# Turning the first chunk of x in two halves, with layer 1 on the first half between

## The chip, the cores and the metric

The kernel runs on one core of a Trainium2 chip. TensorE (PE) multiplies, ScalarE (ACT) and VectorE (DVE) work on tiles in SBUF and PSUM, GpSimd (POOL) makes constants, and SyncE (SP) issues nearly all transfers. The metric is the device time of one execution, in microseconds (us); less is better.

## The reference

A dense layer with GELU and a second dense layer, in bf16, for x of 2048 rows and 448 columns, w1 of 448 x 1792, w2 of 1792 x 448:

```python
h = jnp.einsum("bsd,df->bsf", x, w1) + b1
h = jax.nn.gelu(h, approximate=True)
return jnp.einsum("bsf,fd->bsd", h, w2) + b2
```

## The kernel before

The 2048 rows of x are cut into four chunks of 512, and a chunk into four tiles of 128. For each chunk, layer 1 makes h transposed (features on partitions) in 14 feature tiles of 128, taken two at a time, so in seven pairs; GELU on ScalarE writes it to `g`; and layer 2 multiplies `g` with w2, two row tiles at a time (one at a time at the very end). VectorE adds b2 and SyncE stores.

The contraction over 448 columns is not a multiple of 128. So it is done in slices of 64 rows: TensorE's array is used as two halves of 64 rows, and two matmuls, one for each feature tile of a pair, run side by side on the two halves. A pair of feature tiles lies in one `unit` of PSUM (two banks, one for each tile). `part_a` of a pair takes one 64-row half of three slices for each tile, `part_b` takes the other half, and last the leftover 64 columns (weights `w1r`). Since both parts add to the same bank from different halves of the array, `part_b` waits until the last matmul of `part_a` is done; the function `roll` puts the `part_b` of the pair before between the two. `w1r` is loaded to partitions 64 to 127, and VectorE copies every second feature tile's weights to the lower half (L341).

Every engine has a list of instructions in the order in which the Python code appends them, and it runs that list in order. Waits are semaphores, made out of named events (`after=`, `event=`). SyncE's queue holds, in this order: x of the first chunk (one transfer, L113), the first piece of w1 (feature tiles 0 to 3), `w1r`, the second piece (4 to 7), the third (8 to 13), w2 in two pieces, b2 spread over the partitions, then the other three chunks of x by transposing transfers.

Layer 1 needs x transposed. Chunks 1 to 3 come transposed. The first chunk is turned on TensorE: seven warming matmuls on constants (L158), then for each of four tiles three transposes out of `xn` and one out of `xr`, in which VectorE has put the last 64 columns twice (`twice`, L165). The four transposes of a tile go to one bank, and VectorE or ScalarE copies them to `xT` (L180). All four tiles are turned, then b1 is turned by one more transpose (L187, copied by L189), and only then layer 1 starts. In the first chunk a tile holds the rows p*4+t (so a partition gets four neighbouring rows of x, 3584 bytes), and the stores of that chunk put them back.

The first two pairs of the first chunk run their `part_a` over the columns 0 to 255 and then 256 to 511, which belong to tiles 0 and 1, and 2 and 3; everything else is 512 wide.

```python
for t0 in (0, HC):
    for item in items:
        item[0](t0, t0 + HC)
```

Of the kernel before, what the change touches and what calls it, by code (L numbers as in the profile page):

```python
# [7 lines left out]
BF16 = mybir.dt.bfloat16  # L8
FP32 = mybir.dt.float32


class Program:

# [3 lines left out]
    def __init__(self, nc, es):  # L17
        self.nc, self.es = nc, es
        self.lists = {e: [] for e in self.COMPUTE + ("sync",)}
        self.sems = {e: es.enter_context(nc.semaphore(f"sem_{e}")) for e in self.COMPUTE}  # L20
        self.count = dict.fromkeys(self.COMPUTE, 0)
        self.where = {}

    def op(self, engine, make, after=(), event=None):
        if event is not None:
            self.count[engine] += 1
            self.where[event] = (f"sem_{engine}", self.sems[engine], self.count[engine])
        self.lists[engine].append((make, tuple(after), self.sems[engine] if event else None, 1))

    def dma(self, engine, make, event, after=()):  # L30
        if event not in self.where:
            name = "dma_" + "_".join(str(p) for p in (event if isinstance(event, tuple) else (event,)))
            self.where[event] = (name, self.es.enter_context(self.nc.semaphore(name)), 0)
        name, sem, n = self.where[event]
        self.where[event] = (name, sem, n + 16)
        self.lists[engine].append((make, tuple(after), sem, 16))

    def barrier(self, engine, after):
        self.lists[engine].append((None, tuple(after), None, 0))

    def emit(self):
        for name in self.lists:
            self._run(getattr(self.nc, name), name)

    def _run(self, eng, name):
        seen = {}
        for make, after, sem, inc in self.lists[name]:
            for event in after:
                key, s, value = self.where[event]
                if seen.get(key, 0) < value:  # L50
                    eng.wait_ge(s, value)
                    seen[key] = value
            if make is None:
                continue
            done = make(eng)
            if sem is not None:
                done.then_inc(sem, inc)


def bass_standalone__dense_activation_gelu__prompt_kernel(  # L60
# [21 lines left out]
    NWARM = 7  # L82

    with ExitStack() as es:
        sb = lambda name, shape, dt: es.enter_context(nc.sbuf_tensor(name, shape, dt))
        xT = sb("xT", [P, KT + 1, S], BF16)
# [3 lines left out]
        xn = sb("xn", [P, STC, D], BF16)  # L90
        xr = sb("xr", [P, STC, P], BF16)
        ident = sb("ident", [P, P], BF16)
        junk = sb("junk", [P, 1], BF16)
        b1n = sb("b1n", [P, P], BF16)
        b1_f = sb("b1_f", [P, NFT], FP32)
        b2_bc = sb("b2_bc", [P, D], BF16)
        g = sb("g", [P, NFT, S], BF16)
# [8 lines left out]
        x0v = x2[0:SC, :].rearrange("(p t) d -> p t d", t=STC)  # L106
        o0v = out2[0:SC, :].rearrange("(p t) d -> p t d", t=STC)


        W1CUTS = (0, 4, 8, 14)  # L110

        def load_x():
            pr.dma("sync", lambda e: e.dma_start(xn[:, :, :], x0v[:, :, :]), "x")  # L113
# [16 lines left out]
        load_x()  # L130
        load_w1(0)
        load_w1r()
# [5 lines left out]
        for c in range(1, NSC):  # L138
            for slot, d0 in enumerate((0, P, 2 * P, D - P)):
                pr.dma("sync", lambda e, c=c, slot=slot, d0=d0: e.dma_start(  # L140
                    xT[:, slot, c * SC:(c + 1) * SC], x2[c * SC:(c + 1) * SC, d0:d0 + P], transpose=True), ("xT", c))
# [5 lines left out]
            base=0, pattern=[[-1, P]], channel_multiplier=1), after=["ident0"], event="ident")  # L147
        pr.op("vector", lambda e: e.memset(b1n[:, :], 0.0), event="b1z")  # L148
# [3 lines left out]


        busy = {}

        def warm(n, cols=SC):
            for _ in range(n):
                pr.op("tensor", lambda e: e.matmul(unit[3][:, 1, 0:cols], lhsT=ones_w, rhs=ones_m[:, 0:cols],  # L158
                                                   start=True, stop=True))

        def stage(t):
            return unit[t // 2][:, t % 2, 0:2 * P].bitcast(BF16)

        def twice(t):
            pr.op("vector", lambda e: e.tensor_copy(  # L165
                xr[:, t, :].rearrange("p (two h) -> p two h", two=2),
                xn[:, t, D3:D].unsqueeze(1).broadcast_to([P, 2, H])), after=["x"], event=("xr", t))

        def turn(t, copier):
            for k in range(KT + 1):  # L170
                src = xn[:, t, k * P:(k + 1) * P] if k < KT else xr[:, t, :]
                need = ["ident", "x"] if k < KT else [("xr", t)]
                pr.op("tensor", lambda e, k=k, src=src: e.transpose(  # L173
                    stage(t)[:, k * P:(k + 1) * P], src, ident[:, :]),
                    after=need, event=("xt", t) if k == KT else None)

            def evac(e):
                o = xT[:, :, t * P:(t + 1) * P]
                i = stage(t).rearrange("p (k s) -> p k s", k=KT + 1)
                return e.copy(o, i) if copier == "scalar" else e.tensor_copy(o, i)  # L180

            pr.op(copier, evac, after=[("xt", t)], event=("xT0", t))
            busy[(t // 2, t % 2)] = ("xT0", t)

        def turn_b1():
            b1T = unit[0][:, 1, 0:H].bitcast(BF16)
            pr.op("tensor", lambda e: e.transpose(b1T, b1n[:, :], ident[:, :]),  # L187
                  after=["b1n", "ident", ("xT0", 1)], event="b1T")
            pr.op("vector", lambda e: e.tensor_copy(b1_f[:, :], b1T[:, 0:NFT]), after=["b1T"], event="b1")  # L189
            busy[(0, 1)] = "b1"  # L190
# [3 lines left out]

        order = [2]
# [9 lines left out]
        serial = [0]  # L205

        def fence():
            serial[0] += 1
            return ("half", serial[0])

        def layer1(c, j):
            u = next_unit()
            c0, c1 = c * SC, (c + 1) * SC
            turned = fence()

            def mm(lo, half, k, t0, t1, first, fin, after, event):
                ft = 2 * j + lo
                rows = slice(half * H, (half + 1) * H)
                lhsT = w1_sb[rows, k, ft * P:(ft + 1) * P] if k < KT else w1r[rows, ft * P:(ft + 1) * P]
                pr.op("tensor", lambda e: e.matmul(  # L220
                    unit[u][:, lo, t0:t1], lhsT=lhsT, rhs=xT[rows, k, c0 + t0:c0 + t1], start=first, stop=fin,
                    skip_group_check=c == 0 and j < 2), after=after, event=event)

            def part_a(t0=0, t1=SC):

                need = free(u) if t0 == 0 else []
                need += [("xT0", t) for t in range(t0 // P, t1 // P)] if c == 0 else [("xT", c), ("xTd", c)]
                for k in range(KT):
                    for lo in (0, 1):
                        after = (need if k == 0 else []) + [("w1", w1_of(2 * j + lo))]  # L230
                        mm(lo, lo, k, t0, t1, k == 0 and t0 == 0, False, after,
                           turned if k == KT - 1 and lo and t1 == SC else None)

            def part_b():
                for k in range(KT + 1):
                    for lo in (0, 1):
                        fin = k == KT
                        mm(lo, 1 - lo, k, 0, SC, False, fin, [turned] if k == 0 else ["w1r", "w1rU"] if fin else [],
                           ("h", c, 2 * j + lo) if fin else None)
                for lo in (0, 1):  # L240
                    ft = 2 * j + lo
                    pr.op("scalar", lambda e, lo=lo, ft=ft: e.activation(  # L242
                        g[:, ft, c0:c1], unit[u][:, lo, :], ACT.Gelu_apprx_tanh,
# [3 lines left out]
            return part_a, part_b  # L247

        def store(c, st, after):
            j = c * STC + st  # L250
            dst = o0v[:, st, :] if c == 0 else out2[j * P:(j + 1) * P, :]
            pr.dma("sync", lambda e: e.dma_start(dst, out_sb[:, j, :]), "out", after=after)

        def layer2(c, tiles, last=False):

            u = next_unit()
            split = len(tiles) == 1
            n = DH if split else D
            turned = fence()

            def mm(ft, lo, half, first, fin, after, event):
                st = tiles[0] if split else tiles[lo]
                j = c * STC + st
                rows = slice(half * H, (half + 1) * H)
                d0 = lo * DH if split else 0
                pr.op("tensor", lambda e: e.matmul(  # L266
# [133 lines left out]
```

## Time and profile before

| what | value |
|---|---|
| median of five timed runs | 94.67 us (94.51 to 95.11) |
| the profiled execution | 95.46 us |
| its span, first to last instruction | 94.1 us |
| TensorE busy | 90.2 us, 96% of the span |
| ScalarE busy | 38.0 us, 40% |
| VectorE busy | 12.3 us, 13% |
| DMA engines, mean busy share 0 to 6.88 us | 0.72, 198 GB/s |
| DMA engines, 6.88 to 9.05 us | 1.07, 361 GB/s |

The profile is of one execution, which was slower than the median of the timed ones; the difference between its time and its span lies ahead of the first and behind the last instruction. A line of the profile names the line of the code, the engine, the operation, output and inputs, and its times; "idle before" is how long the engine did nothing just before, and the releaser is what ended that. `w_sb` in the profile stands for both `w1_sb` and `w2_sb` (numbers are dropped from names), `u` for the PSUM units. An instruction of L220 is layer 1, one of L266 layer 2. Matmuls are pipelined, so their lengths overlap; the distance between their starts tells the speed.

### The profile page before, as it was taken

The numbers are of one execution on the slowest core, as the hardware profiler recorded it, in microseconds if no ns is written. First come the engines' busy times: TensorE is split into PE (matmuls) and PEld (weight loads), VectorE is DVE, ScalarE is ACT, GpSimd is POOL, SyncE is SP. The second block draws the span as 40 slices with busy tenths as digits, with TensorE's granted clock in tenths as the row PEclk, the third lists the DMA queues.
The fourth block names the chain that finished last, engine by engine and source line by source line (L and its number), as shares of the span: only waits on it lengthen the run. The fifth ranks groups of instructions, "written<-read, shape, count | busy, mean of one in ns | idle before, by whom it ended". The sixth has DMA issues, their size and how long they took to land.

```text
span 94.1 us, 2049 instructions
## 1 busy us (share of the span) xinstructions
PE 90.2 (96%) x933; PEld 46.6 (50%) x933; DVE 12.3 (13%) x29; ACT 38.0 (40%) x61; POOL 1.1 (1%) x7
## 2 busy tenths in 40 slices
PE   6969999999999999999999999999999999999990
PEld 2446444454554444454544444455544444475890
DVE  0141001000136000000136000000134000000421
ACT  3340878810000878810000878810000878810001
POOL 4000000000000000000000000000000000000000
PEclk9999999999999999999999999999999999999999
DMA  2989999855937100000032000000032000000023
GB/s 58 320 224 367 380 319 68 163 107 113 61 64 196 49 0 0 7 0 0 0 101 89 11 0 0 3 7 0 0 98 88 9 0 7 0 0 7 12 85 98
DMA packets 12260, 7.32 MB, mean 78 GB/s; under 512 B 6940, under 2 KB 12060, under 8 KB 12252
## 3 DMA queue, kind: packets, MB, share of 16 engines
q1 hardware_dynamic: 12224, 7.20, 32.8%
q8 instruction: 7, 0.11, 0.6%
q10 hardware_dynamic: 28, 0.00, 0.0%
q14 instruction: 1, 0.01, 0.0%
HBM read 3.79 MB, written 1.84 MB: 60 GB/s over the span
## 4 chain that ended last, share of the span: by engine, by line
PE 90%; DMA 6%; SPq 0%; DVE 0%; issue 0%
PE u L266 45%; PE u L220 45%; DMA w_sb<-in_w_dram 6%; SPq L113 0%; DVE out_sb L305 0%; PE u L273 0%
## 5 line engine op out<-in xcount | busy, mean ns | idle before, releaser
L242 ACT ACTIVATE g<-u,b_f 128x512 bf16<-128x512 f32 x56 | 35.0, 686 | 41.3 <-PE u L220 41.3
L266 PE MATMUL u<-w_sb,g 64*128 64x448 bf16 (+1 forms) x504 | 43.2, 328 | 0.0
L220 PE MATMUL u<-xT,w_sb 64*128 64x512 bf16 (+1 forms) x348 | 40.9, 369 | 0.9 <-DMA w_sb<-in_w_dram 0.9
L266 PEld LDWEIGHTS u<-w_sb,g 64*128 64x128 bf16 x504 | 24.5, 94 | 18.4
L220 PEld LDWEIGHTS u<-xT,w_sb 64*128 64x128 bf16 x348 | 16.9, 94 | 20.0 <-DMA w_sb<-in_w_dram 1.0
L290 DVE TENSOR_TENSOR out_sb<-u,b_bc 128x448 bf16<-128x448 f32 x14 | 8.1, 620 | 61.3 <-PE u L266 61.3
L220 PE MATMUL u<-xT,w1r 64*128 64x512 bf16 x56 | 10.6, 376 | 0.0
L220 PEld LDWEIGHTS u<-xT,w1r 64*128 64x128 bf16 x56 | 2.7, 94 | 3.3
L308 ACT CAST out_sb<-u 128x224 bf16<-128x224 f32 x1 | 0.3, 346 | 9.2 <-PE u L266 9.2
L158 PE MATMUL u<-const-bfloat16-1.0 128*128 128x512 bf16 x7 | 3.1, 627 | 0.8 <-PEq L385 0.8
L180 ACT COPY xT<-u 128x512 bf16<-128x512 bf16 x2 | 1.2, 586 | 2.2 <-PE u L173 2.2
L158 PEld LDWEIGHTS u<-const-bfloat16-1.0 128*128 128x128 bf16 x7 | 0.9, 138 | 2.1 <-issue 2.1
L151 ACT ACT_TABLE_LOAD x1 | 1.3, 1283 | 1.6 <-DVE b1n L148 1.6
L173 PE MATMUL u<-ident,xn 128*128 128x128 bf16 x12 | 1.8, 302 | 0.1
L173 PEld LDWEIGHTS u<-ident,xn 128*128 128x128 bf16 x12 | 1.3, 139 | 1.0 <-issue 1.0
L361 DVE COPY xT<-xT 64x512 bf16<-64x512 bf16 x3 | 0.9, 289 | 3.8 <-DMA xT<-in_x_dram 3.7
L173 PE MATMUL u<-ident,xr 128*128 128x128 bf16 x4 | 1.1, 283 | 0.0
L357 DVE COPY b_z<-b_bc 1x448 bf16<-1x448 bf16 x1 | 0.3, 268 | 6.5 <-DMA b_bc<-in_b_dram 6.5
L165 DVE COPY xr<-xn 128x128 bf16<-128x128 bf16 x4 | 0.6, 190 | 3.0 <-DMA xn<-in_x_dram 3.0
L180 DVE COPY xT<-u 128x512 bf16<-128x512 bf16 x2 | 0.9, 426 | 0.7 <-PE u L173 0.7
L298 DVE TENSOR_TENSOR out_sb<-u,b_bc 128x448 bf16<-128x448 f32 x1 | 0.6, 625 | 1.7 <-PE u L266 1.7
L341 DVE COPY w1r<-w1r 64x896 bf16<-64x896 bf16 x1 | 0.4, 420 | 1.6 <-DMA w1r<-in_w_dram 1.6
(16 smaller groups left out, 3.4 us busy)
## 6 DMA issues: line engine op xcount, KB each, us to landing
out_dram<-out_sb SPq DMA_DIRECT2D x16, 112.0 KB, 1.7
w_sb<-in_w_dram SPq DMA_DIRECT2D x2, 784.0 KB, 9.7
w_sb<-in_w_dram SPq DMA_DIRECT2D x2, 384.0 KB, 6.0
w_sb<-in_w_dram SPq DMA_DIRECT2D x1, 576.0 KB, 7.4
xn<-in_x_dram SPq DMA_DIRECT2D x1, 448.0 KB, 3.2
w1r<-in_w_dram SPq DMA_DIRECT2D x1, 224.0 KB, 6.1
xT<-in_x_dram SPq DMA_TRANSPOSE x12, 4.2
b_bc<-in_b_dram SPq DMA_DIRECT2D x1, 112.0 KB, 9.0
```

The source lines that it names most:

```text
L151: pr.op("scalar", lambda e: e.activation(junk[:, :], one, ACT.Gelu_apprx_tanh))
L158: pr.op("tensor", lambda e: e.matmul(unit[3][:, 1, 0:cols], lhsT=ones_w, rhs=ones_m[:, 0:cols], start=True, stop=True))
L165: pr.op("vector", lambda e: e.tensor_copy(xr[:, t, :].rearrange("p (two h) -> p two h", two=2), xn[:, t, D3:D].unsqueeze(1).broadcast_to([ ...
L173: pr.op("tensor", lambda e, k=k, src=src: e.transpose(stage(t)[:, k * P:(k + 1) * P], src, ident[:, :]), after=need, event=("xt", t) if k ...
L180: return e.copy(o, i) if copier == "scalar" else e.tensor_copy(o, i)
L220: pr.op("tensor", lambda e: e.matmul(unit[u][:, lo, t0:t1], lhsT=lhsT, rhs=xT[rows, k, c0 + t0:c0 + t1], start=first, stop=fin, skip_group ...
L242: pr.op("scalar", lambda e, lo=lo, ft=ft: e.activation(g[:, ft, c0:c1], unit[u][:, lo, :], ACT.Gelu_apprx_tanh, bias=b1_f[:, ft:ft + 1], s ...
L266: pr.op("tensor", lambda e: e.matmul(unit[u][:, lo, 0:n], lhsT=g[rows, ft, j * P:(j + 1) * P], rhs=w2_sb[rows, ft, d0:d0 + n], start=first ...
L290: pr.op("vector", lambda e, lo=lo, j=j: e.tensor_tensor(out=out_sb[:, j, :], in0=unit[u][:, lo, 0:D], in1=b2_bc[:, :], op=ALU.add), after= ...
L298: pr.op("vector", lambda e: e.tensor_tensor(out=out_sb[:, j, :].rearrange("p (two h) -> p two h", two=2), in0=unit[u][:, :, 0:DH], in1=b2_ ...
L341: pr.op("vector", lambda e: e.tensor_copy(odd(slice(0, H)), odd(slice(H, P))), after=["w1r"], event="w1rU")
L361: pr.op("vector", lambda e, cs=cs: e.tensor_copy(xT[0:H, KT, cs], xT[H:P, KT, cs]), after=[("xT", c + 1)], event=("xTd", c + 1))
```

## The change

The first chunk is turned in two halves. Tiles 0 and 1 of x come as transfers of their own (rows t*128 to t*128+127, 896 bytes for each partition), then the first piece of w1, then tiles 2 and 3 in one transfer. TensorE runs five warming matmuls, turns tiles 0 and 1, runs two more warming matmuls of 256 columns, then `a` of the pairs 0 and 1 on columns 0 to 255, and only then turns tiles 2 and 3. The steps that follow are written out: the other half of the array for these 256 columns (without `w1r`), `a` on columns 256 to 511, the `w1r` step on columns 0 to 255, `a` of pair 2, and then `b` of the pairs 0 and 1 on columns 256 to 511. From pair 3 on the order is as before.

b1 is no longer turned by TensorE: VectorE turns it by four 32x32 block transposes in SBUF and one copy. ScalarE copies tiles 0 and 2, VectorE tiles 1 and 3. The helper `mm` remembers which half of the array last wrote each bank, and makes a matmul of the other half wait for it, bank by bank. Layer 2 of chunks 0 to 2 takes its first parts as feature tiles 0 to 9 of both row-tile pairs, then 10 to 13 of both. The stores of the first chunk write rows in their natural order.

```diff
-    NWARM = 7
+    NWARM = 5
...
-        load_x()
-        load_w1(0)
+        def load_x(t0, t1):
+            pr.dma("sync", lambda e: e.dma_start(
+                xn[:, t0:t1, :], x2[t0 * P:t1 * P, :].rearrange("(t p) d -> p t d", p=P)), ("x", t0))
...
+        load_x(0, 1)
+        load_x(1, 2)
+        load_w1(0)
+        load_x(2, 4)
         load_w1r()
         load_w1(1)
...
+        def turn_b1():
+            for q in range(4):
+                pr.op("vector", lambda e, q=q: e.transpose(
+                    b1t[32 * q:32 * q + 32, :], b1n[:, 32 * q:32 * q + 32]), after=["b1n"], event=("b1t", q))
+            pr.op("vector", lambda e: e.tensor_copy(b1_f[:, :], b1t[:, 0:NFT]),
+                  after=[("b1t", q) for q in range(4)], event="b1")
...
+        def mm(u, lo, half, cols, lhsT, rhs, start, stop, after, event=None, skip=False):
+
+            after = list(after)
+            before = side.get((u, lo))
+            if start:
+                before = None
+            if before is not None and before[0] != half:
+                after.append(before[1])
...
         warm(NWARM)
-        for t, copier in enumerate(("vector", "scalar", "vector", "scalar")):
-            if t % 2 == 0:
-                twice(t)
-                twice(t + 1)
-            turn(t, copier)
+        twice(0)
+        twice(1)
+        turn(0)
+        turn(1)
+        evac_half(0)
+        turn_b1()
+        warm(2, HC)
+        L = [Layer1(0, j) for j in range(NPAIR)]
+        L[0].a(0, HC)
+        L[1].a(0, HC)
+        twice(2)
+        twice(3)
+        turn(2)
+        turn(3)
+        evac_half(1)
...
+        for j in (0, 1):
+            for k in range(KT):
+                L[j].step("b", k, 0, HC)
+        L[0].a(HC, SC)
+        L[1].a(HC, SC)
+        for j in (0, 1):
+            L[j].step("b", KT, 0, HC)
+        L[2].a()
+        L[0].b(HC, SC)
+        L[1].b(HC, SC)
+        for j in range(3, NPAIR):
+            L[j].a()
+            L[j - 1].b()
+        L[-1].b()
...
+            head, tail, every = range(0, 10), range(10, NFT), range(NFT)
+            p = Layer2(c, (0, 1))
+            if c + 1 < NSC:
+                q = Layer2(c, (2, 3))
+                for part in (head, tail):
+                    p.part("a", part)
+                    q.part("a", part)
+                p.part("b", every)
+                q.part("b", every)
```

## The prediction

> **What bounds the kernel now.** I read the chain that ended last first, then the timeline of the start, then the waits.
>
> The chain in order of time (start us, length us, what):
>
> ```profile
> 1.19 5.64 DMA w_sb<-in_w_dram
> 6.83 0.05 issue
> 6.88 10.76 PE u L220 x110
> 17.64 10.59 PE u L266 x112
> 28.24 10.58 PE u L220 x98
> ```
>
> From 6.88 us the chain never leaves TensorE until the last output copy: 85.1 us of matmuls without a hole (a later layer 1 takes 10.58 us, a layer 2 10.59). Only the 6.88 us ahead of them can shrink, and the chain says that they end with the first part of w1. The timeline of that stretch (start, length, engine, line, operation, idle before):
>
> ```profile
> 0.77 3.15 PE L158 MATMUL u<-const-bfloat16-1.0 128*128 128x512 bf16 x7 [0.77 <-PEq L385]
> ...
> 4.03 0.48 PE L173 MATMUL u<-ident,xn 128*128 128x128 bf16 x3
> ...
> 5.81 0.22 PE L187 MATMUL u<-ident,b1n 128*128 128x128 bf16 x1
> 5.88 0.59 ACT L180 COPY xT<-u 128x512 bf16<-128x512 bf16 x1 [0.21 <-PE u L173]
> ...
> 6.88 2.13 PE L220 MATMUL u<-xT,w_sb 64*128 64x256 bf16 x30 [0.86 <-DMA w_sb<-in_w_dram]
> 7.79 0.42 DVE L341 COPY w1r<-w1r 64x896 bf16<-64x896 bf16 x1 [1.56 <-DMA w1r<-in_w_dram]
> ```
>
> TensorE itself is busy until 6.02, then idles 0.86. So the wait for w1 is worth at most 0.86 us while 16 transposes and that of b1 stand ahead of the matmuls. The groups give the price of layer 1's small pieces and what they waited for:
>
> ```profile
> L220 PE MATMUL u<-xT,w_sb 64*128 64x256 bf16 x24 | 1.5, 270 | 0.9 <-DMA w_sb<-in_w_dram 0.9
> ```
>
> The clock: a 128x512 warming matmul starts every 0.43 us and a transpose every 0.107 us until about 5.58; later a pair of 512-wide half-row matmuls starts every 0.216 and a pair of 256-wide ones every 0.109. So the array runs at half speed until 5.58.
>
> One thing decides how to read this: the profiled execution took 95.46 us (94.1 span, 1.36 around it), the median of the timed runs is 94.67, 0.79 less. The landing record of the first w1 piece has 14 of its 16 parts by 4.98 us and two stragglers, 6.09 and 6.84. Without stragglers the matmuls could start at 6.02, 0.86 earlier. That is nearly the whole difference, so I estimate that timed runs are already bound by TensorE's own prologue, not by w1.
>
> **What the Trainium skill says.** "TensorE: Matmul & The Clock Gate", Part 1: the array is at half clock until a free-running window of about 3.4 us has been busy; the trace agrees as to the half speed and the switch at 5.58, 4.8 us after the first matmul. "DMA: Bandwidth & Descriptors", Queues, rings and completion order: each engine takes descriptors in ring order, and a transfer is done only when all its engines are; the stragglers fit. "VectorE: DVE Perf Modes", The three transpose paths: 311 ns for a 128x128 VectorE transpose in 32x32 blocks; no run shows one yet.
>
> **The change, part by part.** I use a marker at which both programs have done the same matmul work: the start of the third pair's first matmuls (20 half-width pairs of layer 1 done, 20 x 0.109 = 2.18 us). Before: 6.88 + 2.18 = 9.06 in the profile, and 6.02 + 2.18 = 8.20 by my estimate for the timed runs. All after the marker is equal work.
>
> *First tiles.* x was 448 KB, 3.2 us to landing. Two tiles of 112 KB come first; a store of 112 KB takes 1.7 us. Bounds for the second tile: 2.9 (issue 1.19 + 1.7) to 3.9 (as before); I take 3.1. Five warming matmuls end at 0.77 + 5 x 0.43 = 2.9. Eight transposes x 0.107 = 0.86: the last starts at 3.85. In before the VectorE copy starts 0.35 after the start of a tile's last transpose and takes 0.43: xT of two tiles is there at 4.63. Matmuls may start at 4.65, against 6.02.
>
> *w1, first piece.* Issued one place later on SyncE (1.65, not 1.19), but with 224 KB less ahead, some 0.7 us of x's transfer: most parts by 4.3, a straggler 5.4 to 6.1. I take 4.65 as the start.
>
> *First half of two pairs.* 6 pairs. Half clock until 5.58 gives 0.93 / 0.215 = 4.3 of them, the other 1.7 cost 0.19: 5.77. The clock costs 0.47 here.
>
> *Turning tiles 2 and 3, now among the matmuls.* Eight transposes that stood in a prologue now stand on the path. At full clock not shown well: between 0.055 (half of 0.107) and 0.107; I take 0.08, so 0.64 (0.44 to 0.86): 6.41. Their x lands behind the first w1 piece, 5.0 to 5.5 without stragglers, covered.
>
> *Then* 6 pairs of the other row half, 0.65: 7.06. VectorE's copy of tile 3 ends at 6.35 + 0.35 + 0.43 = 7.13, so 0.07 of waiting; ScalarE's copy of tile 2 (0.59) is earlier. 6 pairs of the second half: 7.78. The new waits between row halves of one bank: a 256-wide matmul lasts 0.27, three pairs (0.33) lie between for most, so 0 to 0.1; for the second pair's w1r step only one pair lies between: 0.27 + 0.05 - 0.11 = 0.2. Two pairs with w1r, 0.22. Sum 8.2 to 8.3.
>
> *w1r and the second w1 piece.* w1r landed at 7.77 (14 parts by 7.02) and its VectorE copy takes 0.42, needed at about 7.8: ready 7.5 to 8.25. The second piece landed at 8.64 (14 parts by 8.12), needed at 8.2 to 8.3. The same bytes are ahead; x in rows of 896 bytes instead of 3584, and two more issues on SyncE of about 0.45 each, put up to 0.2 to 0.4 on both. Without stragglers this hides, just.
>
> *b1.* Off TensorE: minus 0.1 (one transpose) from the prologue. VectorE gets four block transposes and a copy, by the page's price 0.3 to 0.6 with the copy, ahead of the copies for tiles 2 and 3: 4.63 + 0.5 = 5.1, before tile 2 is needed at 5.77. Hidden; if x comes late it stays hidden too.
>
> *Later.* SyncE's transposing loads and b2 issue up to 0.9 later; the first are needed at 28 us and were there before 18.7: nothing. ScalarE's first GELU comes 0.5 to 1 later than 9.27; it works 1.27 of every 1.51 us, and catches up before layer 2, where the last GELU outputs are needed after 20 feature tiles of work, not 12: nothing. The outputs' rows and the split of layer 2 keep 56 pairs of matmuls and at least four pairs between half switches: nothing.
>
> Sum: marker at 8.25, that is 0.8 below the profiled execution's 9.06 (95.46 - 0.8 = 94.65 profiled) but about equal to the 8.20 that I estimate for the timed runs: 94.67 + 0.05, about 94.7.
>
> **The rivals.**
> *A. As summed, about equal: 94.7* (94.3 to 95.1 for itself). What is won by the earlier start (1.37) is spent: half clock 0.47, transposes 0.64, waits 0.3. Chance 0.43.
> *B. Faster: the timed runs before did wait for w1 as the profile shows*, the 0.79 lies elsewhere, and the new order removes that wait: 94.67 - 0.75 = 93.9; or the clock rises earlier. For it: the chain names w1. Against: no room is left then for the 0.79, and stragglers would delay the new kernel as well (w1 at 6.1, x behind it, marker about 9.2). Chance 0.22.
> *C. Slower: the clock stays down for another window.* The new prologue has holes: before tile 1, and from 4.25 (end of two half warming matmuls) to 4.65 or, with a straggler, to 6.1. If the busy share falls short the switch comes 3.41 later, at 8.99: first half 1.29, transposes 0.86, next 1.29 and most of the next at half speed, marker 9.6: 94.67 + 1.4 = 96.1. It decides when the share in the window ending at 5.58 is too small; the first window (TensorE busy 1.4 of 3.41, 41%) was, the second (97%) was not; mine is about 89%. Against it, then. Chance 0.15.
> *D. Slower: a transfer takes the place of the old wait.* w1r or the second w1 piece lands 0.2 to 0.4 later through small rows and later issues, on top of a landing as the profile had: marker 8.85 to 9.1, 95.3 to 95.6. The change would then not do what it says. For it: data move at 180 to 270 GB/s between 4.5 and 6.5 us, less than later, whatever the order. Chance 0.20.
>
> **Numbers.** 0.5% of 94.67 is 0.47 us, about what a measurement tells from none. Same is A, 0.43; faster B, 0.22; slower C and D, 0.35. The range goes from B to C, 93.9 to 96.1, leaving the far side of each.
>
> **What would show it.** Right: the first L215 matmul starts near 4.65; the transposes of tiles 2 and 3 take about 0.64 between two bursts; the third pair starts at 8.2 to 8.3; no hole after it. C shows as 256-wide pairs every 0.215 us past 6; D as TensorE idle before the third pair or before the w1r step, put down to DMA. A hole in the later chunks, or layer 2 above 10.59 us, would make the sum wrong altogether.

## The result: a little slower, and where the half microsecond went

The changed kernel stands at 1.0059 of the kernel before, 95% interval 1.0033 to 1.0084. On a median of 94.68 us (47 runs) that is 0.56 us, so 95.24 us. Its median over all 28 runs is 96.51 us, but 16 of these took 96.4 us or more (of the kernel before 3 of 47) and lie outside the ratio, by which the text below compares. The profiled execution took 95.65 us with a span of 94.3 (before: 95.46 and 94.1).

The chain that ended last, of the kernel after (start us, length us, what):

```profile
1.65 0.43 SPq L130
2.08 0.04 issue
2.12 4.80 DMA xn<-in_x_dram
6.92 0.05 issue
6.97 0.69 PE u L342 x8
7.65 84.50 PE u L215 x913
```

Before, the chain went through the first piece of w1 until 6.83. Now it goes through tiles 2 and 3 of x, until 6.92, and only after these and their eight transposes does TensorE run without a hole. In this execution the wait was not removed. It was given to another transfer.

The timeline of the same stretch of the kernel after:

```profile
4.32 0.89 DVE L179 STREAM_TRANSPOSE b1t<-b1n 32x32 bf16<-32x32 bf16 x4
...
5.55 0.55 PEld L215 LDWEIGHTS u<-xT,w_sb 64*128 64x128 bf16 x12 [1.67 <-DMA w_sb<-in_w_dram]
5.56 0.83 PE L215 MATMUL u<-xT,w_sb 64*128 64x256 bf16 x12 [1.19 <-DVE b_f L181]
...
6.94 0.30 DVE L335 COPY xr<-xn 128x128 bf16<-128x128 bf16 x2 [1.42 <-DMA xn<-in_x_dram]
...
6.97 0.34 PE L342 MATMUL u<-ident,xn 128*128 128x128 bf16 x3 [0.58 <-DMA xn<-in_x_dram]
...
7.58 1.49 PE L215 MATMUL u<-xT,w_sb 64*128 64x256 bf16 x24
...
9.25 1.17 PE L215 MATMUL u<-xT,w_sb 64*128 64x512 bf16 x12
```

Layer 1 does start earlier, at 5.56 against 6.88. (The page puts the wait of the matmul down to VectorE's bias copy; the code has no such wait there, and the weight load's row names w1, which landed at 5.51.) At 6.39 the first burst of six pairs is over, and TensorE idles for 0.58 us until tiles 2 and 3 have landed. The third pair's first matmul, the prediction's marker, is at 9.25; before it was at 9.06. What follows is the same work in the same time, as a table by stretch shows (start:end, length, busy time of TensorE and its weight loads, ...), first the kernel after, then the one before:

```profile
6.20:6.97 0.77, 0.19 (x5) 0.01 (x1) 0.03 (x1) 0.00 (x0) 0.00 (x0) 1.00 1.03 241
6.97:7.58 0.61, 0.61 (x8) 0.44 (x9) 0.27 (x2) 0.12 (x1) 0.00 (x0) 1.00 1.09 339
7.58:9.25 1.67, 1.67 (x31) 1.36 (x31) 0.84 (x2) 0.47 (x1) 0.00 (x0) 1.00 1.05 365
9.25:94.30 85.05, 82.85 (x888) 55.05 (x886) 10.24 (x20) 34.98 (x57) 0.00 (x0) 1.00 0.26 61
```

```profile
9.06:94.10 85.04, 82.85 (x879) 42.55 (x875) 10.24 (x20) 35.37 (x57) 0.00 (x0) 1.00 0.28 61
```

From the marker to the end it is 85.05 and 85.04 us. So the reordered layer 2, the waits bank by bank and the new rows of the stores cost nothing, and the whole question lies in the first nine microseconds. It also gives a rule for the runs without a trace: a span is the marker plus 85.05, a time is the span plus some 1.35.

By this rule 94.68 us puts the marker of the kernel before at 8.28, so its layer 1 at 6.10, and 95.24 us puts the marker of the changed kernel at 8.84. This is an estimate, and it says that the traced execution of the changed kernel (9.25) was later than most. Against 8.28 its account is: layer 1 starts 0.54 earlier, then come 0.58 of idle time, 0.61 of turning, and 2.50 for the 20 half-width pairs (0.83 and 1.67) where the kernel before needs 2.18. The head start is smaller than the turning alone, which the kernel before does while w1 is still on its way.

### The profile page after: what moved, and what is told of

Same layout as the page of the kernel before. It is cut to its first block, busy times and chain, and to the rows that moved or that the text cites. A ratio compares the mean times of both kernels' runs of the same rounds, so it can differ in the third digit from the quotient of the medians.

```text
span 94.3 us, 2088 instructions
## 1 busy us (share of the span) xinstructions
PE 89.6 (95%) x948; PEld 58.9 (62%) x948; DVE 13.2 (14%) x33; ACT 37.6 (40%) x61; POOL 1.1 (1%) x7
## 4 chain that ended last, share of the span: by engine, by line
PE 90%; DMA 5%; SPq 1%; DVE 0%; issue 0%
PE u L215 90%; DMA xn<-in_x_dram 5%; SPq L148 1%; PE u L342 1%; SPq L130 0%; DVE out_sb L323 0%
## 5 line engine op out<-in xcount | busy, mean ns | idle before, releaser
L215 PE MATMUL u<-xT,w_sb 64*128 64x512 bf16 (+1 forms) x360 | 41.9, 362 | 1.2 <-DVE b_f L181 1.2
L215 PEld LDWEIGHTS u<-w_sb,g 64*128 64x128 bf16 x504 | 30.8, 94 | 12.0
L215 PEld LDWEIGHTS u<-xT,w_sb 64*128 64x128 bf16 x360 | 22.3, 94 | 15.2 <-DMA w_sb<-in_w_dram 1.7
L215 PE MATMUL u<-xT,w1r 64*128 64x512 bf16 (+1 forms) x60 | 11.8, 363 | 0.0
L215 PEld LDWEIGHTS u<-xT,w1r 64*128 64x128 bf16 x60 | 3.9, 94 | 2.4
L190 PE MATMUL u<-const-bfloat16-1.0 128*128 128x512 bf16 (+1 forms) x7 | 2.9, 564 | 0.8 <-PEq L440 0.8
L179 DVE STREAM_TRANSPOSE b1t<-b1n 32x32 bf16<-32x32 bf16 x4 | 0.8, 199 | 0.1
```

The lines of the kernel that those rows point to most:

```text
L179: pr.op("vector", lambda e, q=q: e.transpose(b1t[32 * q:32 * q + 32, :], b1n[:, 32 * q:32 * q + 32]), after=["b1n"], event=("b1t", q))
L190: pr.op("tensor", lambda e: e.matmul(unit[2][:, 1, 0:cols], lhsT=ones_w, rhs=ones_m[:, 0:cols], start=True, stop=True))
L215: o = pr.op("tensor", lambda e: e.matmul(unit[u][:, lo, cols], lhsT=lhsT, rhs=rhs, start=start, stop=stop, skip_group_check=skip), after=a ...
```

## The experiments

Twelve kernels were run, each against the kernel before. Four of the names begin with b, and start from the kernel before; the others start from the changed one. From the traces in which the clock was at full speed by about 6 us: when the last part of three transfers had landed, and when the third pair started (us).

| kernel | rows of x, bytes | first w1 piece, last part | x tiles 2, 3 | second w1 piece | third pair starts | span |
|---|---|---|---|---|---|---|
| before | 3584 | 6.83 | 3.89 | 8.64 | 9.06 | 94.1 |
| after | 896 | 5.51 | 6.92 | 8.61 | 9.25 | 94.3 |
| b_warm2 | 3584 | 5.95 | 3.95 | 8.26 | 8.31 | 93.4 |
| b_dveb1 | 3584 | 6.17 | 3.82 | 7.99 | 8.47 | 93.5 |
| a_fill | 896 | 5.26 | 6.42 | 8.64 | 8.75 | 93.8 |
| a_fill_nox23 | 896 | 5.59 | (not waited for) | 8.67 | 8.71 | 93.8 |
| a_fill_noturn | 896 | 5.29 | (not waited for) | 8.65 | 8.69 | 93.8 |
| a_two_fill | 1792 | 4.53 | 5.62 | 7.96 | 8.72 | 93.8 |
| a_two_short | 1792 | 4.78 | 6.03 | 8.01 | 8.36 | 93.4 |

In the traces of a_xfirst, a_onex, b_split, b_x2 and a_cold the clock was at half for longer, which changes the starts of matmuls; from them landings and the clock are read.

### Is the kernel before bound by its own prologue? (b_warm2)

```diff
                 turn_b1()
+                warm(2)
```

> The kernel before with two more 512-wide warming matmuls on TensorE behind the transpose of b1 (2 x 0.21 to 0.43 us of TensorE time ahead of the first matmul of layer 1). If timed runs of the kernel before are bound by TensorE's own prologue, as the prediction estimated, the time rises by 0.4 to 0.6 us. If they wait for w1 with 0.86 us of idle time as the profile shows, nothing changes (within 0.1 us).

Measured: 1.0019 (0.9997 to 1.0041), about 0.2 us, and the interval reaches from nothing to 0.39. In its trace the chain no longer names w1 at all:

```profile
5.09 0.45 PE u L173 x5
5.55 0.13 PE u L187
5.68 0.43 PE u L158 x2
6.11 10.79 PE u L220 x110
```

Here the first w1 piece landed at 5.95 and TensorE's prologue set the start, although it had two matmuls more than before. So in this execution the kernel before would have started at 5.68 or, with w1, at 5.95. The prediction's reading, that the profiled execution of before was one with a late w1 and that the runs are not like it, holds in part at most: by the middle of the interval half of the added 0.43 us shows, and the other half lies in waiting that is there anyway. This trace also shows what waits behind it: the third pair started at 8.31, 0.05 after the second piece of w1 had landed.

### Order and transfers apart (a_onex, b_split), and the bias (b_dveb1)

a_onex keeps the changed order but loads x in one transfer, rows as before (stores to match):

```diff
-        load_x(0, 1)
-        load_x(1, 2)
+        load_x(0, 4)
         load_w1(0)
-        load_x(2, 4)
```

> The order of the changed kernel alone: x of the first chunk in one transfer of 3584-byte rows as before, seven warming matmuls, and everything else as changed. If the split transfers are what the change costs (tiles 2 and 3 at 6.1 to 6.9 us instead of 3.5 to 3.9), TensorE no longer waits between its two bursts and the time is within 0.3 us of the kernel before (ratio 0.997 to 1.003). If the order is the cost (turning on the path, new waits), it stays 0.4 to 0.6 us slower than before.

b_split is the opposite, the kernel before with the changed kernel's transfers of x:

```diff
-        load_x()
+        load_x(0, 1)
+        load_x(1, 2)
         load_w1(0)
+        load_x(2, 4)
```

> The transfers of the changed kernel alone: the kernel before with x as tile 0, tile 1, the first piece of w1, tiles 2 and 3 in 896-byte rows; all four tiles are still turned ahead of layer 1. If tiles 2 and 3 land at 6.1 to 6.9 us as in the changed kernel, layer 1 starts at about 7.3 to 7.8, and the time is 1.0 to 1.6 us above before. If the late landing comes from the changed kernel's order and not from the transfers, it lands near 4 us and the time is level with before.

Measured: the order alone 1.0049 (1.0023 to 1.0074), the transfers alone 1.0056 (1.0022 to 1.0090), both together 1.0059. The order alone should have been level if the late tiles were the only cost: it is not. It came out as the other branch of its expectation has it, 0.4 to 0.6 us slower through the order itself. With x in one piece, nothing is there earlier than before (x at 3.95, w1's first piece at 6.66), so there is no head start, and the turning of two tiles still comes after w1. The expectation of b_split missed. The transfers alone should have cost 1.0 to 1.6 us and cost 0.2 to 0.85: tiles 2 and 3 landed at 6.37, late as in the changed kernel, and layer 1 started at 7.09, earlier than I had worked out, 0.67 after the turning of these tiles had begun. That two parts of 0.5 us add up to 0.56 says that they are not two costs in a row. The landings fit this reading: the split makes tiles 2 and 3 late, but with it the last part of w1's first piece landed at 5.0 to 5.6 in six traces, and at 5.95 to 6.83 in the four in which x went ahead of it in one transfer (before, b_warm2, b_dveb1, a_onex). That is the head start that the order lacks alone. No run shows the sum itself.

b_dveb1 has the four block transposes of the change in the kernel before:

```diff
-            pr.op("tensor", lambda e: e.transpose(b1T, b1n[:, :], ident[:, :]), ...
+            for q in range(4):
+                pr.op("vector", lambda e, q=q: e.transpose(b1t[32 * q:32 * q + 32, :], b1n[:, 32 * q:32 * q + 32]), ...
```

> The bias part alone: the kernel before with b1 turned by VectorE in four block transposes and a copy. They take about 1.0 us on VectorE, ready near 7.1, before the first GELU at 9.3, and hidden. TensorE's prologue is 0.1 to 0.2 us shorter: 0 to 0.2 us faster than before; a slower kernel would say that VectorE's time is not hidden.

Measured: 1.0005 (0.9980 to 1.0031), no difference. The bias part is neither gain nor loss. This trace, of an execution of 94.86 us, also shows TensorE waiting for w1, whose last part landed at 6.17:

```profile
6.30 2.13 PE L221 MATMUL u<-xT,w_sb 64*128 64x256 bf16 x30 [0.43 <-DMA w_sb<-in_w_dram]
```

### Is it the wait for tiles 2 and 3? (a_xfirst, a_fill, a_fill_nox23, a_fill_noturn)

a_xfirst issues tiles 2 and 3 ahead of the first piece of w1:

```diff
-        load_w1(0)
         load_x(2, 4)
+        load_w1(0)
```

> The changed kernel with tiles 2 and 3 of x issued ahead of the first piece of w1 instead of behind it. If the idle time before tiles 2 and 3 are turned (0.58 us in the profile after) is what the change costs, it goes, and the kernel is 0.3 to 0.6 us faster than the changed one, level with the kernel before. The rival, that transposes among the matmuls and the clock are the cost, gives no change or, since w1 lands 0.4 us later, a slower kernel.

Measured: no ratio; its six times spread from 95.57 to 98.46 us, none below the median of the kernel before. The trace shows one reason. Tiles 2 and 3 landed at 4.45, but the first piece of w1 at 6.73, and TensorE's idle time in front of layer 1 is now 2.05 us. From its chain:

```profile
2.12 4.61 DMA w_sb<-in_w_dram
6.73 0.05 issue
6.78 0.83 PE u L215 x12
```

And the row of the granted clock, in 40 slices of 2.4 us, shows what such a hole can do:

```profile
PEclk9996699999999999999999999999999999999999
```

The clock had risen at 4.39 and fell at 7.81 for 3.41 us. In the 3.41 us before the fall TensorE was busy for 1.36. The same fall stands in the trace of b_split, after a hole from 4.6 to 6.4 (1.57 of 3.41 us busy), and in that of b_x2 (fell at 7.68, 1.35 of 3.41 us busy).

a_fill closes the hole behind the first transposes:

```diff
-        warm(2, HC)
+        warm(4)
```

> The changed kernel with four 512-wide warming matmuls where it has two 256-wide ones, so that TensorE is busy from 3.7 to about 5.4 us instead of to 4.2. Clock theory: the hole in TensorE's prologue leaves the array at half clock in a part of the executions; filled, the times draw together and the median falls by 0.3 to 1.3 us. Transfer theory: the median stays, or rises by up to 0.2 us where the filler ends after w1 has landed.

Measured: 1.0084 (1.0062 to 1.0106). The median over all runs fell from 96.51 to 95.63, as the clock theory has it, but the ratio did not fall; if anything the filler costs 0.2 us (the intervals overlap), as far as it reaches past the landing of w1 (5.26 in the trace; layer 1 started at 5.58). So what the ratio of the changed kernel measures is not the clock.

a_fill_nox23 and a_fill_noturn take work out of a_fill. The first turns tiles 2 and 3 out of the data of tiles 0 and 1, so nothing waits for the late transfer; the second does not turn them at all.

```diff
-                src = xn[:, t, k * P:(k + 1) * P] if k < KT else xr[:, t, :]
+                src = xn[:, t % 2, k * P:(k + 1) * P] if k < KT else xr[:, t, :]
```

> The filled kernel (four 512-wide warming matmuls behind tiles 0 and 1), in which the tiles 2 and 3 are turned out of the data of tiles 0 and 1, so that nothing waits for the late transfer (it still runs; the rows 256 to 511 of the result are those of other rows). The filled kernel stood at 1.0084. If TensorE's wait for tiles 2 and 3 (0.33 us between its bursts in the filled kernel's profile, 0.85 in the changed one's) is part of the cost, the time falls by 0.3 to 0.5 us, to 1.003 to 1.005. If the wait only hides a later one for w1r or the second piece of w1, it stays at 1.007 to 1.009.

```diff
-        twice(2)
-        twice(3)
-        turn(2)
-        turn(3)
-        evac_half(1)
...
+        for t in (2, 3):
+            pr.op("gpsimd", lambda e, t=t: e.memset(xT[:, :, t * P:(t + 1) * P], 0.0), event=("xT0", t))
```

> The filled kernel without the turning of tiles 2 and 3: their part of xT is set to zero by GpSimd early on, so TensorE goes from its first burst straight to the second (left out: eight transposes, two copies, two doublings; rows 256 to 511 are wrong). If the transposes on the path cost what the prediction took (0.64) on top of the wait for x, the time falls by 0.9 to 1.1 us against the filled kernel, to 0.996 to 0.999. If w1r or the second w1 piece binds right behind, it falls by 0.4 or less.

Measured: 1.0055 (1.0031 to 1.0080) and 1.0033 (1.0000 to 1.0067). Against 1.0084 that is 0.27 us for the wait, just short of what was expected, and 0.48 us for the wait and all the turning, about half of what was expected (0.9 to 1.1). The interval of the first overlaps that of a_fill from 1.0062 to 1.0080, so its 0.27 us is not told from nothing; the 0.48 us is, by little, and its size is rough. The other branch of the second expectation, 0.4 us or less because w1r or the second piece of w1 binds right behind, is nearer. The timeline of a_fill_noturn shows where the rest went:

```profile
7.69 0.42 DVE L374 COPY w1r<-w1r 64x896 bf16<-64x896 bf16 x1 [2.17 <-DMA w1r<-in_w_dram]
...
8.17 0.39 PE L217 MATMUL u<-xT,w1r 64*128 64x256 bf16 x3 [0.17 <-DVE w1r L374]
8.69 0.87 PEld L217 LDWEIGHTS u<-xT,w_sb 64*128 64x128 bf16 x12 [0.41 <-DMA w_sb<-in_w_dram]
8.69 1.04 PE L217 MATMUL u<-xT,w_sb 64*128 64x512 bf16 x10
```

Without any turning TensorE was through its bursts at 7.7, stood for the copy of w1r until 8.16, and then for the second piece of w1 until 8.69. In a_fill_nox23 it is the same: the second piece landed at 8.67, the third pair started at 8.71. This is a floor under the whole change. Whatever is won ahead of the third pair, it starts when the second piece of w1 is there. With the changed kernel's transfers that was 8.6 to 8.7 in the four traces of the table, and 8.27 and 8.36 in those of b_split and a_cold.

### Rows and number of transfers (b_x2, a_two_fill, a_two_short)

a_two_fill loads tiles 0 and 1 as one transfer and 2 and 3 as another, each partition taking two neighbouring rows of x, 1792 bytes (with six warming matmuls, then three; stores to match):

```diff
-        load_x(0, 1)
-        load_x(1, 2)
+        load_x(0, 2)
         load_w1(0)
         load_x(2, 4)
...
-                xn[:, t0:t1, :], x2[t0 * P:t1 * P, :].rearrange("(t p) d -> p t d", p=P)), ("x", t0))
+                xn[:, t0:t1, :], x2[t0 * P:t1 * P, :].rearrange("(p t) d -> p t d", p=P)), ("x", t0))
```

> The filled kernel with tiles 0 and 1 of x as one transfer of 1792-byte rows, then the first piece of w1, then tiles 2 and 3 as one of 1792-byte rows (six warming matmuls, then three behind the first transposes). If the row size or the extra transfer makes w1 and the later tiles land late, they land 0.3 to 0.5 us earlier than in the filled kernel and the time is 1.000 to 1.005 of before. If only the order of the bytes counts, it stays at 1.006 to 1.009.

a_two_short has one warming matmul behind the first transposes instead of three:

> The kernel with tiles 0 and 1 as one transfer of 1792-byte rows, w1, then tiles 2 and 3, with one 512-wide warming matmul behind the first transposes instead of three. In the run with three, w1 had landed at 4.53 us and the filler held layer 1 back to 5.74. If the filler binds, layer 1 starts near 5.2 and the time is 0.2 to 0.4 us lower, 0.997 to 1.000 of before. If the second piece of w1 (7.96 there, 8.6 in the changed kernel) or the clock binds, it stays at 1.000 to 1.004.

Measured: 1.0017 (0.9990 to 1.0044) and 1.0008 (0.9983 to 1.0034). The first lies clear of a_fill's 1.0084 (1.0062 to 1.0106): with the same interleaved order, two transfers of longer rows in place of three give back 0.6 us. The table shows it transfer by transfer: w1's first piece at 4.53 and 4.78 against 5.26 to 5.59, tiles 2 and 3 at 5.62 and 6.03 against 6.42 and 6.92. This does not show that the rows are the reason. With one transfer fewer ahead of them both are also issued 0.46 us earlier, w1 at 1.19 instead of 1.65 and tiles 2 and 3 at 1.65 instead of 2.12. From issue to landing w1's first piece took 3.3 and 3.6 us, against 3.4 to 3.9 in the six traces with three transfers, and tiles 2 and 3 took 4.0 and 4.4 against 4.0 to 4.8. So most of the gain is the earlier issue, and an effect of the row length alone is not shown. In a_two_fill nothing on TensorE's way waits for a transfer any more (chain):

```profile
3.55 1.01 PE u L343 x8
4.56 1.25 PE u L189 x3
5.81 0.76 PE u L214 x12
6.57 0.55 PE u L343 x8
7.12 84.50 PE u L214 x913
```

In a_two_short layer 1 starts at 5.10, the tiles 2 and 3 hold it up once more until 6.08, and the third pair starts at 8.36:

```profile
1.19 0.42 SPq L130
1.60 0.05 issue
1.65 4.38 DMA xn<-in_x_dram
6.03 0.05 issue
6.08 0.68 PE u L343 x8
```

Its ratio lies in the second branch of its expectation, but for another reason: what holds it up is tiles 2 and 3, not the second piece of w1 (8.01) or the clock (which rose at 4.83). It is level with the kernel before, not ahead of it; neither version beats it.

b_x2 has the same two transfers in the order of the kernel before, both ahead of w1:

```diff
-        load_x()
+        load_x(0, 2)
+        load_x(2, 4)
         load_w1(0)
```

> The kernel before with x in two transfers instead of one, tiles 0 and 1 (1792-byte rows) and then 2 and 3, both ahead of w1. If it is small rows or the number of transfers that slows the first microseconds, w1 lands up to 0.5 us later and the time rises by 0 to 0.5 us. If only the place behind w1 makes tiles 2 and 3 late, the first two tiles are turned 0.5 us earlier and the time falls by 0.2 to 0.5 us.

Measured: 1.0106 (1.0061 to 1.0150), the slowest but for a_cold. It is worse than either expectation. In its trace the parts of w1's first piece landed in two groups, half by 5.66 and half between 6.62 and 7.38. So longer rows alone do not make w1 early; the place in the queue counts as well. Why half the parts came so late is not explained.

### What half clock would cost (a_cold)

```diff
-    NWARM = 5
+    NWARM = 2
...
-        warm(2, HC)
```

> The changed kernel with two warming matmuls at the start instead of five and none behind the first transposes. Clock theory: 256-wide pairs of layer 1 start every 0.215 us instead of 0.109 until the clock rises, at about 9 us, and the time is 1.0 to 1.8 us above the changed kernel's. If the clock rises by elapsed time or by any activity, nothing changes.

Measured: 1.0247 (1.0174 to 1.0320), 1.8 us above the changed kernel. Layer 1's first burst in the timeline, 1.46 us for twelve matmuls where the changed kernel has 0.83:

```profile
5.18 1.46 PE L215 MATMUL u<-xT,w_sb 64*128 64x256 bf16 x12 [1.24 <-DMA w_sb<-in_w_dram]
```

The clock rose at 10.6 us. So the warming matmuls are not decoration, and the prediction's price for case C, 1.4 for a rise at 8.99, is of the right order; a rise at 8.99 itself was not run.

## The prediction against the runs, step by step

The forecast was 94.7 us, 93.9 to 96.1, with "about equal" the likeliest; the ratio gives 95.24, 0.09% past the bound of equal. The range held, but it reached from the gain of case B to the loss of case C, so that it held says little for the sum. 95.24 lies outside case A's own 94.3 to 95.1 and just short of D's 95.3 to 95.6. The likeliest case was 0.5 us off, and the error is in one kind of term, the landings. In the trace the marker is 1.00 us later than the 8.25 of the sum: 0.91 for the start of layer 1 and 0.58 for tiles 2 and 3, less 0.29 for the first burst, 0.03 for the turning and 0.17 for the rest. The three that go the other way were not foreseen, so in part it is luck that the sum came so near.

**Right.** That the kernel before can gain at most the prologue, and that the page's 0.86 us of waiting for w1 is not what most runs have: 94.68 less 1.35 and 85.05 puts their marker at 8.28, where 8.20 was estimated. (That they do not wait for w1 at all, as the estimate has it, is not right; see case B.) The turning on the path: 0.64 was taken, 0.61 measured. The copies of tiles 0 and 1: 4.63 taken, 4.40 measured. The pairs and the new waits after the turning: 14 pairs take 1.53, the stretch was 1.67, so 0.14 for waits where up to 0.3 was allowed. Everything after the marker: nothing, as said.

**Wrong: the start of layer 1.** For w1's first piece the working had two ends, 4.3 for most parts and 5.4 to 6.1 for a straggler, and took 4.65. The last part came at 5.0 to 5.6 in all six traces with the changed kernel's order of transfers, and no straggler made it so: in the trace of after 14 of the 16 parts had landed only by 5.05. I had reasoned that 224 KB less ahead of w1 makes it 0.7 us earlier, and against the 14 parts at 4.98 of before nothing was won, with w1 issued 0.46 us later. What came forward is the last part alone, from 5.95 to 6.83 in the four traces with x in one transfer ahead of it.

**Wrong: tiles 2 and 3, "covered".** They were put at 5.0 to 5.5 and costed at nothing. They landed at 6.92 in the changed kernel and 6.42 in a_fill; TensorE stood idle for 0.58 us in the one and 0.06 in the other, and taking the wait away from a_fill gave 0.27 us, not told from nothing. This term was missing from the sum. It was case D in kind, a transfer in the place of the old wait, though D had named w1r and the second w1 piece, which stand one step further on. D's reason, a slow stretch between 4.5 and 6.5 us whatever the order, held by half: in the changed kernel 346 to 385 GB/s moved until 5.5, and 182 to 210 from there to 6.5.

**Wrong: small rows and more transfers.** Small rows and later issues were allowed 0.2 to 0.4 us in the last two transfers, and nothing in tiles 2 and 3. Going from 896 to 1792 bytes, with one transfer fewer, moved w1's first piece by 0.3 to 1.1 us and the time by 0.6. The issue alone is 0.46 us earlier, and for the rows by themselves nothing is shown.

**Wrong in size, hidden all the same: the bias.** 0.3 to 0.6 us from the Trainium skill's 311 ns ("VectorE: DVE Perf Modes", The three transpose paths). The trace has 0.89 for the four block transposes and 0.17 for the copy, 1.06: the page's figure is for a whole 128x128, and here four separate instructions of 0.2 each do a quarter of that. It ended at 5.5, before tile 2 was needed, and b_dveb1 shows no cost.

**Not needed: the half clock in the sum.** 0.47 was charged for the first burst at half speed. In the trace of after the twelve matmuls took 0.83 at full speed, because they started so late. It was paid in waiting instead.

**Case B**, that the runs before did wait for w1, was refuted by b_warm2 in part only. TensorE waited 0.43 us for w1 in the trace of b_dveb1, and in that of b_warm2 w1 landed 0.27 after the point at which the prologue without the two added matmuls ended. **Case C** is not what the ratio measures. The fall of the median over all runs from 96.51 to 95.63 in a_fill speaks for it in the executions that the ratio leaves out; none of these was traced for the changed kernel, so it is not shown.

**Not drawn as a consequence: the floor.** The working says of the second piece of w1 that it "hides, just". With that piece at 8.3 to 8.7, no order ahead of it could bring the changed kernel below the marker of 8.28 that the kernel before has in its runs, and a gain was hardly to be had. Even without any turning or wait for x (a_fill_noturn) the kernel was 0.3 us slower than before, with an interval from nothing to 0.63. How the 0.56 us split between this floor and the wait for tiles 2 and 3 stays open: no run moved the second piece alone, and it also landed at 8.64 in the profiled execution of before.

## What to carry to other kernels

An earlier start is worth what the next transfer allows: before moving work forward, list each later transfer with the time at which it will then be needed, and cost the one that is needed sooner than it lands. A load cut into tiles so that the first can start sooner also has more transfers, and everything queued behind it is issued later (here by 0.46 us for each). Work that stood in a prologue while a transfer was on its way is not free once it stands behind that transfer: the turning of two tiles cost 0.61 us of TensorE's time there. When a transfer's landing record has a tail of one or two late parts, plan with the tail.

## What the runs showed of the hardware

The clock of TensorE did not only rise late, it fell again: in a_xfirst, b_split and b_x2 it went to half for 3.41 us after a stretch of 3.41 us with TensorE busy for 1.36, 1.57 and 1.35 of them, transposes counted. The Trainium skill ("TensorE: Matmul & The Clock Gate", Part 1) speaks of an idle window for this; here a window with 40 to 46% of work in it fell as well.

A transfer of 112 KB from HBM landed 2.1 us after its issue; one of 448 KB with rows of 3584 bytes took 3.2. Of the 16 parts of one transfer, the last came up to 1.9 us behind the fourteenth.
